# A spectral and FFN block: leftover rows of a DFT on 32-row tiles, a mirrored weight, and new orders of work

## The chip, the cores and the metric

The kernel runs on one core of a Trainium2 chip. Its engines work side by side, each on its own queue of instructions in program order: TensorE (PE) multiplies matrices, VectorE (DVE), ScalarE (ACT) and GpSimd (POOL) work element by element, and SyncE (SP) issues most of the DMA transfers. A matmul first loads its stationary operand, the weights, into the array (PEld in the profile), then streams the moving operand through it, and leaves its result in PSUM. Another engine has to copy it out to SBUF before the next stage can use it; these copies are called evictions here. The metric is the device time of one execution in microseconds (us).

## The reference

One block with a modulation: two halves, each a normalization, an affine from the condition `c`, a transform, and a gated sum.

```python
mod = (silu(c) @ w_mod).reshape(c.shape[0], 6, 1, -1)
sa, ca, ga, sb, cb, gb = (mod[:, i] for i in range(6))
h = layernorm(x) * (1 + ca) + sa
x = x + ga * irfft2(rfft2(h) * (w_r + 1j * w_i))
h = layernorm(x) * (1 + cb) + sb
x = x + gb * ((silu(h @ w_gate) * (h @ w_up)) @ w_down)
```

`x` is 1 x 2048 x 640 (S x D) in bf16, the transforms run over both axes, so the spectrum is 2048 x 321. The FFN is 1728 wide. The sums run in float32, tables and intermediate values are bf16.

## The kernel before

The two-dimensional transform is cut into small ones. D = 640 is 5 x 128: 128 positions with five residues r, and for the frequencies 65 columns l. S = 2048 is 16 tiles of 128 rows. The kernel has four stages, and the order inside each of the first three is a string of steps, `plan`, written by hand: each word is a function and a unit number, and the steps are issued to their engines in that order.

**Phase 1** (lines 268 to 415) works on 16 tiles t of x. `T` transposes a tile on TensorE (`turn`, L283), `h` copies it out (L286), `G` multiplies it by itself for the variance (L290), `d`, `p` and `r` make the reciprocal deviation, `s` scales the table G by it (L310, mostly POOL), `B` is the DFT along D (L317), `Z` its eviction with the mean taken out (L322, DVE), `S` the DFT along the rows of a tile (L330, L331) and `A` its eviction into `A_sb` (L335, ACT). `A_sb` holds, for each of the 65 columns l, NI = 160 numbers (tile, real or imaginary part, r). `ca` and `cb` scale the DFT table by the modulation; `ms` (L375), `sacs` (L379), `mh` (L386 to L390) and `sh` (L395) make the transform of the shift sa, `dsa`, which has five rows.

**The seam.** Phase 2 needs `A_sb` the other way round, in units u of four columns l: 4 x 160 = 640 values, or five blocks of 128, in `B2all`. Units 0, 1 and 16 are transposed on TensorE (`T` L436, `t` L442), units 2 to 15 by seven DMA transposes of two units each (`B`, L429), which SP issues. Since 160 is more than 128 rows, a column's values lie over two blocks, and each unit has its own cuts at rows 32, 64 and 96.

**Phase 2** (lines 417 to 627) is the short DFT across the tiles, the product with w_r and w_i, and the way back. For unit u, `X` (`stage_x`) multiplies the five blocks by ten variants of a table K: two matmuls of 320 columns (L456, L457), two small ones of ten by the weight `first`, which add the shift `dsa` (L459), and four of 160 (L461 to L464). Where a block holds parts of two columns, zero rows in K cut them apart. `Xe` evicts X (L471, ACT). `P` multiplies by the weights in one function, first 48 rows from `Wb`, then 32 from `Wq` (both at L489, DVE). `Y` sums the products with a unit matrix as weights (L503, L507) and `y` evicts it (L514), `E` is the inverse short DFT (L525 to L538) and `e` its eviction into `Ep` (L543, L548). `m` writes mirrored negative columns of `Ep` (L264, DVE).

`Wq` is W with its rows mirrored across partitions: `J` multiplies `Wb` by an exchange matrix `jrev` on TensorE (L585), `Je` copies it out (L588), `Jn` negates a third part. The mirror along l isn't done there: `P` reads `Wq` with a step of -1 along its last axis. `W0` to `W3` write the negative of `Wb` in four pieces of columns (L264). All these steps stand in the plan of phase 2, between `T`, `X` and `B`.

**Phase 3** takes the spectral output back to rows: `s` (`s1inv`, L646), `V` (its eviction, L653), `d` (`dinv`, L659), `x` (the sum with x, L662), then the second normalization (`n`, `q`, L666 and L670), `T` (turns in pairs), `f` (affine, L702 and L704). `sb`, `cb` and `mb` are the last three columns of the modulation, 25 small matmuls each (L231), and `sx`, `cx`, `mx` their evictions. The first units of the FFN (`gA`, then `g`, `z`, `m`) are interleaved at the end.

**The FFN** (from `ffn13` L725 and `ffn_mm` L738 on) multiplies by the gate and up weights, applies Silu on ACT (L743), the product on DVE (L747), and multiplies by the down weights (L860). The last 64 of 1728 rows, `down13` (L847), run on 64-row tiles of the array, where two matmuls can lie side by side. The end of the output has two matmuls at L857.

Phases 2 and 3 share four PSUM slots of two banks each (`slot`, `ring`). A step that needs a slot waits for the eviction of the one that had it.

Loads are issued by SP in the order of lines 188 to 211, before all plans:

```python
for g in range(0, NT, 2):
    if g:
        nc.sync.dma_start(x_sb[:, g:g + 2, :], x_v[:, g:g + 2, :])
    if g:
        nc.sync.dma_start(Gtab[:, g - 2:g], G_dram[:, g - 2:g])
```

and then `w_sa`, W, K, KI, eight small loads that replace parts of row 0 of W, the weights of the gate ga, and Rinv.

Of the kernel before, what the change touches and what calls it, by code (L numbers as in the profile page):

```python
# [19 lines left out]
NI = 160  # L20
# [10 lines left out]
def _tables():  # L31
# [16 lines left out]
    T["G"] = (5 * np.stack([np.cos(g), -np.sin(g)], axis=2)).astype(_NPBF)  # L48
# [29 lines left out]
    K = np.zeros((128, 17, NI))  # L78
    M = fwd(F)
    for v, (p0, p1, i0) in enumerate(((0, 128, 0), (0, 32, 128), (32, 128, 0), (0, 64, 96),  # L80
                                      (64, 128, 0), (0, 96, 64), (96, 128, 0), (0, 128, 32))):
        K[p0:p1, v] = M[i0:i0 + p1 - p0]
    turn = np.exp(-2j * np.pi * np.arange(NR) / 10.0)
    M = fwd(F * turn)
    K[96:128, 8], K[:, 9] = M[0:32], M[32:160]
    I = inv(F, (1, 1, 1, 1, 1))
    K[:, 10] = I[0:128]
    K[:, 11] = inv(F, (0.5, 1, 1, 0, 0))[0:128]
    K[:, 12] = inv(F * turn, (1, 1, 0.5, 0, 0))[0:128]
    for j in range(4):  # L90
        K[j::4, 13 + j] = I[128:160]
    ph = 2 * np.pi * np.outer(np.arange(NR), np.array([2, 1, 0, 3, 4])) / 5.0
    ph64 = ph + (2 * np.pi * np.arange(NR) / 10.0)[:, None]
    cs = np.stack([np.cos(ph), np.sin(ph), -np.sin(ph), np.cos(ph64), -np.sin(ph64)], axis=1)
    T["K"] = np.concatenate([K[:, :10].reshape(128, -1), np.broadcast_to(cs.reshape(1, -1), (128, 125)), np.zeros((128, 3))],
                            axis=1).astype(_NPBF)
    T["KI"] = np.ascontiguousarray(K[:, 10:]).astype(_NPBF)
# [4 lines left out]
NK = 10 * NI + 128  # L102
# [3 lines left out]
def adaln_block_kernel(  # L106
# [26 lines left out]
    Kv = Ktab[:, 0:10 * NI].rearrange("p (v q) -> p v q", q=NI)  # L133
    cs_v = Ktab[:, 10 * NI:10 * NI + 125].rearrange("p (r f) -> p r f", r=NR)
# [10 lines left out]
    rstd1 = const.tile([P, NT], F32, name="rstd1")  # L145
# [4 lines left out]
    sacs = const.tile([P, NR, 25], BF16, name="sacs")  # L150
# [8 lines left out]
    HB = 12  # L159
    early = big.tile([P, 2 * NC5 * D + HB * 660 + D], BF16, name="early", tag="ep")  # L160
    wm_ca = early[:, 0:NC5 * D].rearrange("p (k n) -> p k n", n=D)
    wm_sa = early[:, NC5 * D:2 * NC5 * D].rearrange("p (k n) -> p k n", n=D)
    hT_all = early[:, 2 * NC5 * D:2 * NC5 * D + HB * 660].rearrange("p (b r q) -> p b r q", b=HB, r=NR)
    c_row = early[0:1, 2 * NC5 * D + HB * 660:]
# [8 lines left out]
    Wq = big.tile([P, 3 * NT * 128 + 4], BF16, name="Wq", tag="wq")  # L173
    Wbr = Wb[:].rearrange("p a k (m l) -> p (a k m) l", m=3)
    Wqp = Wq[:, 0:3 * NT * 128].rearrange("p (a q) -> p a q", a=3)
    Wqr = Wq[:, 0:3 * NT * 128].rearrange("p (r l) -> p r l", l=64)
# [7 lines left out]
    nc.vector.memset(Wq[:, 3 * NT * 128:], 0.0)  # L184
    nc.vector.memset(Wqp[:, 1, 0:2048:64], 0.0)
# [4 lines left out]
    nc.sync.dma_start(x_sb[:, 0:2, :], x_v[:, 0:2, :])  # L190
    nc.sync.dma_start(wm_ca[:, 0:4], wm_v[:, 0:4, D:2 * D])
    nc.sync.dma_start(Rp, R_dram)
    nc.sync.dma_start(wm_ca[:, 4:5], wm_v[:, 4:5, D:2 * D])
    for g in range(0, NT, 2):
        if g:
            nc.sync.dma_start(x_sb[:, g:g + 2, :], x_v[:, g:g + 2, :])
        if g:
            nc.sync.dma_start(Gtab[:, g - 2:g], G_dram[:, g - 2:g])
    nc.sync.dma_start(Gtab[:, NT - 2:NT], G_dram[:, NT - 2:NT])
    nc.sync.dma_start(wm_sa, wm_v[:, :, 0:D])  # L200
    ws = [w.rearrange("(k2 k1) l -> k1 k2 l", k1=P) for w in (A_w_i, A_w_r)]
    for a in (1, 0):
        nc.sync.dma_start(Wb[:, a, :, 0:321], ws[a])
    nc.sync.dma_start(Ktab[:], K_dram)
    nc.sync.dma_start(KIt[:], KI_dram)
    for a in (1, 0):
        for m in (65, 193):
            for lo, hi, k in ((0, 15, 1), (15, 16, 0)):
                nc.sync.dma_start(Wb[0:1, a, lo:hi, m:m + 63], ws[a][0:1, k:k + hi - lo, m:m + 63])
    nc.sync.dma_start(wm_g[:, :, 0:D], wm_v[:, :, 2 * D:3 * D])  # L210
    nc.sync.dma_start(Rinv_sb[:], Rinv_dram)
# [8 lines left out]
    nc.gpsimd.memset(first[0:NR, 0:1], float(S))  # L220
# [5 lines left out]
    nc.scalar.activation(warm[:], eps_t[:], ACT.Silu)  # L226

# [32 lines left out]
    def negate(lo, hi, eng):  # L260
        eng(Wbr[:, 96:144, lo:hi], Wbr[:, 0:48, lo:hi])

# [3 lines left out]
    A_sb = big.tile([P, NL, NT, 2, NR], BF16, name="A_sb", tag="a")  # L266
    A_fl = A_sb[:].rearrange("p l t c r -> p (l t c r)")
    with tc.tile_pool(name="ph1", bufs=3) as ph1, \
# [4 lines left out]
        nc.gpsimd.memset(ones[:], 1.0)  # L273
        nc.vector.memset(Gt[:, 130:131], 1.0)
# [10 lines left out]
        def turned(t):  # L285
            (nc.vector.tensor_copy if t in HT_DVE else nc.scalar.copy)(hT_all[:, t % HB, :, 0:128], held.pop(("t", t)))  # L286

        def sums(t):
            for r in range(NR):
                nc.tensor.matmul(Gt[:, 0:130], lhsT=hT_all[:, t % HB, r, 0:128], rhs=hT_all[:, t % HB, r, 0:130],  # L290
                                 start=(r == 0), stop=(r == NR - 1))
# [15 lines left out]
        def gscale(t):  # L307
            Gss[t] = ph1.tile([P, 3, 128], BF16, name="Gs", bufs=6)
            e = nc.vector if t in S_DVE else nc.gpsimd
            e.tensor_scalar(Gss[t][:, 0:2], Gtab[:, t], rstd1[:, t:t + 1], None, ALU.mult)  # L310
            e.tensor_scalar(Gss[t][:, 2], Gtab[:, t, 1], rstd1[:, t:t + 1], -1.0, ALU.mult, ALU.mult)

        def dfwd(t):
            z = hold("z")
            held["z", t] = z
            for r in range(NR):
                nc.tensor.matmul(z[:, 128 * r:128 * r + 128], lhsT=hT_all[:, t % HB, r, 0:128], rhs=Rs[:, r, :],  # L317
                                 start=True, stop=True)
# [14 lines left out]
        def acopy(t):  # L333
            i = held.pop(("a", t)).rearrange("p (c x) -> p c x", c=2)[:, :, 0:325].rearrange("p c (r l) -> p l c r", r=NR)
            (nc.vector.tensor_copy if t in A_DVE else nc.scalar.copy)(A_sb[:, :, t, :, :], i)  # L335
# [42 lines left out]
        def sa_cs(_):  # L378
            nc.vector.tensor_tensor(sacs[:], cs_v, cps.unsqueeze(2).to_broadcast([P, NR, 25]), ALU.mult)  # L379

        def mod_sahat(_):
            sv = sacs[:].rearrange("p r (f m) -> p r f m", f=5)
            for cc, a, b, e in ((0, 0, 1, 3), (1, 2, 0, 4)):
                o = Tt[0:NR, 340 + NL * cc:340 + NL * cc + NL]
# [7 lines left out]
        def sa_out(_):  # L392
            sh = Tt[0:NR, 340:340 + 2 * NL].rearrange("p (c l) -> p c l", c=2).unsqueeze(2).to_broadcast([NR, 2, NR, NL])
            e5 = identb[0:NR, 0:NR].unsqueeze(1).unsqueeze(3).to_broadcast([NR, 2, NR, NL])
            nc.vector.tensor_tensor(dsa[0:NR, :, :, 0:NL], sh, e5, ALU.mult)  # L395

        HT_DVE, A_DVE, S_DVE, T_RING = (0,), (), (14,), (1, 3)
        GROUP = {0: 2, 2: 2, 4: 2, 6: 2, 8: 2, 10: 2, 12: 2, 14: 2}
        plan = (
# [549 lines left out]
```

## Time and profile before

| what | us |
|---|---|
| runs: lowest, median, highest of three | 269.31, 269.8, 271.63 |
| profiled execution, first to last instruction | 267.3 |
| phase 1 from the first full TensorE work (10.24 to 33.30): TensorE busy | 22.72 of 23.06 |
| FFN (85.50 to 264.00): TensorE busy | 178.50 of 178.50 |
| last copy and store (264.00 to 267.30): TensorE busy | 0.01 of 3.30 |

Of the profiled execution only the span is given; its own device time is not listed apart from it. The granted clock of TensorE was 0.999 over the whole span. The times of one stage are read like this: the windows give busy time per engine in a stretch, and what is missing to the stretch's length on TensorE is time in which it stood. The chain of waits then says which engine or transfer it stood for. In phase 1 DVE was busy for 20.75 us, ACT for 18.25 and POOL for 18.02 of 23.06 us.

### The profile page before, as it was taken

How to read it: one execution, taken by the hardware profiler on the slowest of the kernel's cores; microseconds unless marked ns; L12 is line 12 of the kernel's file. 1: busy time of each engine (PE TensorE's matmuls, PEld its weight loads, DVE VectorE, ACT ScalarE, POOL GpSimd, SP SyncE). 2: the span in 40 equal slices, each digit the busy share in tenths (PEclk: the TensorE clock that was granted, in tenths of full speed). 3: DMA queues.
4: the chain of work that ended last, by engine and by line, in shares of the span. 5: the costliest groups of instructions: out<-in, count | busy, mean ns of one | idle time of the engine just before them, and what ended most of it. 6: DMA issues, size and time to landing. Idle time of an engine off the chain costs nothing.

```text
span 267.3 us, 5300 instructions
## 1 busy us (share of the span) xinstructions
PE 258.3 (97%) x2180; PEld 166.6 (62%) x2180; DVE 148.3 (56%) x335; ACT 120.3 (45%) x216; POOL 26.0 (10%) x53
## 2 busy tenths in 40 slices
PE   6899999999989999999999999999999999999995
PEld 5688868998987445466644447654445664444663
DVE  2799989999598377773333352523344442333152
ACT  5599678988797598230122223022222203222000
POOL 3378800000010011100000000000000000000000
PEclk9999999999999999999999999999999999999999
DMA  7999399993696100050100013110005021000011
GB/s 252 325 332 326 111 271 172 308 395 111 196 379 218 35 13 0 0 98 28 64 19 12 0 33 65 53 59 10 2 0 98 3 73 34 10 2 0 0 52 49
DMA packets 36734, 28.12 MB, mean 105 GB/s; under 512 B 19429, under 2 KB 34022, under 8 KB 36582
## 3 DMA queue, kind: packets, MB, share of 16 engines
q1 hardware_dynamic: 36698, 27.79, 35.6%
q8 instruction: 17, 0.28, 0.4%
q14 instruction: 7, 0.06, 0.1%
q10 hardware_dynamic: 12, 0.00, 0.0%
HBM read 20.37 MB, written 2.62 MB: 86 GB/s over the span
## 4 chain that ended last, share of the span: by engine, by line
PE 86%; DMA 4%; ACT 3%; DVE 3%; SPq 2%; issue 1%; ACTq 0%
PE gu L738 42%; PE oa L860 21%; DMA x_sb<-in_A_x_dram 2%; PE yps L503 2%; DVE late L662 2%; DMA B2all<-A_sb 2%; PE gu L725 2%; PE z L317 2%; PE aps L330 2%; PE t1ps L283 1%; PE aps L331 1%; PE va L646 1%; PE gps L290 1%; PE mg_ps L231 1%; SPq L429 1%; PE oa L847 1%
## 5 line engine op out<-in xcount | busy, mean ns | idle before, releaser
L747 DVE TENSOR_TENSOR AT<-gu,sg 128x512 bf16<-128x512 f32 x52 | 35.9, 690 | 62.2 <-ACT sg L743 62.2
L738 PE MATMUL gu<-h2T_all,Wg 128*128 128x512 bf16 x260 | 64.6, 379 | 0.0
L738 PE MATMUL gu<-h2T_all,Wu 128*128 128x512 bf16 x260 | 64.6, 379 | 0.0
L743 ACT ACTIVATE sg<-gu 128x512 f32<-128x512 f32 x52 | 31.0, 597 | 69.8 <-PE gu L738 69.6
L860 PE MATMUL oa<-late,AT 128*128 128x320 bf16 x403 | 56.1, 299 | 0.0
L860 PEld LDWEIGHTS <-AT 128*128 128x128 bf16 x429 | 40.8, 98 | 17.2 <-issue 1.4
L738 PEld LDWEIGHTS <-Wu 128*128 128x128 bf16 x260 | 25.4, 98 | 30.7
L738 PEld LDWEIGHTS <-Wg 128*128 128x128 bf16 x260 | 25.1, 98 | 29.3
L874 DVE TENSOR_TENSOR xo<-oa,late 128x320 bf16<-128x320 f32 x31 | 20.0, 694 | 29.8 <-PE oa L847 16.7
L727 ACT ACTIVATE sg<-gu 64x512 f32<-64x512 f32 x4 | 2.4, 590 | 36.2 <-PE gu L725 36.2
L662 DVE SCALAR_TENSOR_TENSOR late<-oab,x_sb 128x640 bf16<-128x640 f32 x16 | 13.9, 890 | 4.8 <-PE oab L659 4.7
L310 POOL TENSOR_SCALAR Gs<-Gtab,rstd 128x256 bf16<-128x256 bf16 x15 | 13.9, 928 | 10.4 <-DVE rstd L305 9.1
L322 DVE SCALAR_TENSOR_TENSOR Z<-rtile,vm,z 128x640 bf16<-128x640 f32 x16 | 13.9, 872 | 0.4 <-PE z L317 0.3
L670 ACT ACTIVATE junk<-late,mean 128x640 bf16<-128x640 bf16 x16 | 13.3, 832 | 0.3
L471 ACT CAST X<-xps 128x640 bf16<-128x640 f32 x16 | 10.7, 696 | 3.3 <-PE xps L464 2.3
L335 ACT CAST A_sb<-aps 128x650 bf16<-128x650 f32 x16 | 11.1, 706 | 2.5 <-PE aps L331 2.3
L286 ACT COPY early<-t1ps 128x640 bf16<-128x640 bf16 x13 | 9.0, 692 | 4.6 <-PE t1ps L283 4.3
L646 PE MATMUL va<-Htab,Ep 128*128 128x128 bf16 x160 | 10.6, 219 | 0.3 <-DVE late L662 0.2
L653 ACT CAST VT<-va 128x640 bf16<-128x640 f32 x16 | 10.5, 705 | 0.5 <-PE va L646 0.4
L646 PEld LDWEIGHTS <-Ep 128*128 128x128 bf16 x160 | 9.7, 118 | 0.6 <-issue 0.5
L503 PE MATMUL yps<-identb,PP 128*128 128x128 bf16 x130 | 9.8, 219 | 0.0
L330 PE MATMUL aps<-Z,Gs 128*128 128x325 bf16 x32 | 9.2, 303 | 0.0
(287 smaller groups left out, 333.8 us busy)
## 6 DMA issues: line engine op xcount, KB each, us to landing
x_sb<-in_A_x_dram SPq DMA_DIRECT2D x8, 320.0 KB, 6.4
out_dram<-xo SPq DMA_DIRECT2D x15, 160.0 KB, 1.8
Wu<-in_B_w_up_dram SPq DMA_DIRECT2D x1, 2080.0 KB, 10.3
late<-in_B_w_down_dram SPq DMA_DIRECT2D x1, 2080.0 KB, 16.5
wm_g<-in_w_mod_dram SPq DMA_DIRECT2D x2, 800.0 KB
Wb<-in_A_w_r_dram SPq DMA_DIRECT2D x1, 1284.0 KB, 11.0
Wb<-in_A_w_i_dram SPq DMA_DIRECT2D x1, 1284.0 KB
Wg<-in_B_w_gate_dram SPq DMA_DIRECT2D x1, 1280.0 KB
```

What stands on the lines that cost most here:

```text
L310: e.tensor_scalar(Gss[t][:, 0:2], Gtab[:, t], rstd1[:, t:t + 1], None, ALU.mult)
L322: nc.vector.scalar_tensor_tensor(Zs[t][:].rearrange("p r q -> p (r q)"), rv, vm[:, t, 1:2], held.pop(("z", t))[:, 0:D], ALU.mult, ALU.add)
L330: nc.tensor.matmul(o, lhsT=Gs[:, a, :], rhs=Z[:, :, 0:NL], start=True, stop=False)
L503: nc.tensor.matmul(yf[:, 128 * j:128 * j + 128], lhsT=PP[:, cp, 0:128] if u == 16 else PP[:, cp, 0:128, j], rhs=identb[:], start=(cp == 0) ...
L646: nc.tensor.matmul(vf[:, 128 * r:128 * r + 128], lhsT=Ep[:, t, 65 - 65 * g:193 - 65 * g, r], rhs=Htab[:, t, g, :], start=(f == 1 and r in ...
L662: nc.vector.scalar_tensor_tensor(x1[:, t, :].rearrange("p (r a) -> p r a", r=NR), VTs.pop(t).rearrange("p (r a) -> p r a", r=NR), 1.0, x_s ...
L670: nc.scalar.activation(junk[:], x1[:, t, :], ACT.Square, scale=-1.0 / D ** 0.5, bias=mean2[:, t, 1:2], accum_out=sq2[:, t:t + 1])
L738: nc.tensor.matmul(o, lhsT=w_[:, c5, fc * 128:(fc + 1) * 128], rhs=h2T_all[:, sc % 2, :, c5, :], start=(c5 == 0), stop=(c5 == NC5 - 1))
L743: nc.scalar.activation(gus[fc][1][:], gus[fc][0][:, 0, :], ACT.Silu)
L747: nc.vector.tensor_tensor(AT[:, fc, :], gu[:, 1, :], sg[:], ALU.mult)
L860: nc.tensor.matmul(o, lhsT=AT[:, fc, tl * 128:(tl + 1) * 128], rhs=Wd_sb[:, fc, h * 320 + d0:h * 320 + d0 + n], start=(fc == 0 and not ear ...
L874: nc.vector.tensor_tensor(xos[tl][:, h * 320:(h + 1) * 320].rearrange("p (a r) -> p a r", r=NR), ps[0][0].rearrange("p (a r) -> p a r", r= ...
```

## The change

**Blocks.** `A_sb` is cut into `A_main`, which holds 128 of a column's 160 values, and `A_rest`, which holds the other 32. `A` writes tiles 0 to 11 into the one and 13 to 15 into the other, and tile 12 by three copies. A unit is then four blocks of 128 in `Bm` and one block in `Bl`, where the 32 leftover rows of four columns lie on top of each other. The DMA transposes of `Bm` have 8 blocks, not 10; two more, `Bl2` (6 blocks) and `Bl8` (8 blocks), bring the leftovers of units 2 to 15. `t` makes two copies.

**X.** `X` takes two units at once, in two PSUM slots. The table K shrinks from ten variants to four.

```diff
+            other = pss["x", u + 1] = slot("xps")
+            for h in range(2):
+                for j in range(4):
+                    mm((xps, other)[j // 2][:, j % 2, NI * h:NI * h + NI], lhsT=Bm[:, (u + h) % 8, j], rhs=Kv[:, 0, :], start=(h == 0), stop=False)
+            for h in range(3):
+                for j in range(4):
+                    g, o = slice(32 * j, 32 * j + 32), (xps, other)[j // 2][:, j % 2, :]
+                    if h == 0:
+                        mm(o[:, 0:2 * NI].rearrange("p (h c q) -> p h c q", h=2, c=2)[:, :, :, 45:50], lhsT=first[g, :],
+                           rhs=dsa[g, :, :, 4 * u + j:4 * u + j + 5:4].rearrange("p c m h -> p h c m"), start=False, stop=False)
+                    else:
+                        mm(o[:, NI * (h - 1):NI * h], lhsT=Bl[g, u + h - 1, :], rhs=Kv[g, 1, :], start=False, stop=(h == 2))
```

That is eight matmuls of 160 columns on the full array, then twelve on 32 rows, in three rounds of four row groups. `first` and `dsa` are repeated in four groups of 32 rows for this: the weights of `mh` are widened from 5 to 128 columns (`sacs` writes 500 values a partition, not 125, into a cleared tile), and `sh` works on 128 partitions with a mask. `Xe u` now evicts one of the two slots, that is two columns of each unit, so a `P` needs both evictions of its pair. X is stored as one tile for two units.

**The mirrored weight.** `J` moves from phase 2 into phase 1 and reads the moving columns backwards, so that `Wq` is mirrored along l too:

```diff
-                nc.tensor.matmul(ps[:, b, :], lhsT=jrev[:], rhs=wv[:, 8 * (h % 2) + 4 * b:8 * (h % 2) + 4 * b + 4, :, 64:128], start=True, stop=True)
+                nc.tensor.matmul(held["j", h][:, 512 * b:512 * b + 512], lhsT=jrev[:],
+                                 rhs=wv[:, 8 * (h % 2) + 4 * b:8 * (h % 2) + 4 * b + 4, :, 127:63:-1], start=True, stop=True)
```

The product is cut into two steps, `P` (48 rows from `Wb`) and `R` (32 rows from `Wq`), and `R` reads with a step of +1. The negations `W0` to `W3` and `Jn` become `N0` and `N1`, 8 x 321 values a partition each, and `N2`, 2048 values:

```diff
+        def negate(i):
+            if i == 2:
+                neg_dve(held["wq"][:, 0], held["wq"][:, 2])
+            else:
+                neg_dve(Wb[:, 2, 8 * i:8 * i + 8, 0:321], Wb[:, 0, 8 * i:8 * i + 8, 0:321])
```

**Loads.** They become steps of the plans. In the order of the queue: x0, ca (four of five parts), x2, ca (the rest), R, x4, G0, x6, G2, G8, x8, x12, x10, G4, x14, G10, G12, G6, W real, W imaginary, one small load of row 0, sa, G14, two small, K between five more small ones; in phase 2 ga, B2, Bl2, B4, Bl8, KI, B6, B8, H, B10, Rinv, B14, B12, sb, Wu, the second half of `wm_g`. The table G is stored so that a load of two tiles is one piece. The copies of turned x in `hT_all` are kept for all 16 tiles, not in a ring of 12, and part of the modulation weights lie where `Wq` will be.

**Engines of the evictions.** One list names those on DVE, all others are on ACT:

```python
ON_DVE = set("Je0 Xe0 Xe8 Xe10 Xe13 Xe14 e12 e16 g15 h0 h4 t1 t16 y2 y4 y14".split())
```

Before, X was evicted on ACT, Y on DVE but for seven odd units, E on ACT but for unit 14 and half of 15, and of J two on DVE.

**Plans.** All three strings are new. The end of phase 1, then the beginning of phase 2, before and after:

```diff
-            "A12 S13 A13 S14 A14 sh S15 A15 "
+            "... s14 Z15 ms1 s15 S13 S14 sacs S15 A13 J2 "
+            "A14 mh N1 A15 J3 J0 N0 Je2 Je3 sh Je0 J1 Je1 N2 "
...
-            "W0 J3 W1 T0 Je3 J2 J0 Je2 t0 Je0 T1 B2 X0 t1 Xe0 ga Jn J1 X1 X2 B4 Xe1 Je1 P0 Xe2 X3 gt X4 Xe3 B6 X5 Y0 P1 Xe4 "
+            "T0 lga t0 T1 ga B2 Bl2 t1 X0 Xe0 X2 Xe1 R1 B4 P1 X4 Xe3 P0 R0 Xe2 Y1 Xe4 y1 Bl8 P3 P2 R2 lKI Xe5 Y0 R3 y0 E1 e1 P4 B6 "
+            "gt B8 Y2 E0 y2 Y3 X6 L3 R4 e0 y3 Y4 R5 P5 Xe6 y4 E2 Xe7 B10 Y5 e2 R6 P6 R7 lRi E3 y5 e3 X8 Y6 E5 Xe8 E4 P7 Xe9 R9 y6 "
```

At the end of phase 2 it now reads `E14 E15 e12 e14 e15 m4 wm m3`: the step `wm`, which loads ACT's table for Silu, stands behind the last eviction of E (before: ahead of `e14`, `e16` and `e15`). Phase 3 begins `sb sx cb s0 s2 cx s1 V0 V2 V1 d0` where it began `sb sx cb cx s0 s1 s2 V0 d0`, has `mb` and `mx` ahead of the turns `T0` and `T1` where they stood between `f1` and the first step of the FFN, `gA` (L725), and has `gA` itself behind the units 2 and 5 of the FFN, and takes the first FFN units in the order 2, 5, 6, 0, 4, 3, 1, 7.

More of the change, by code (lines that the diff above doesn't have):

```diff
@@ L149, in adaln_block_kernel @@
     sc_col = const.tile([P, NC5], BF16, name="sc_col")
-    sacs = const.tile([P, NR, 25], BF16, name="sacs")
+    mask5 = const.tile([P, NR], F32, name="mask5")
     dsa = const.tile([P, 2, NR, 68], BF16, name="dsa")
@@ L219, in adaln_block_kernel @@
     nc.gpsimd.memset(first[:], 0.0)
-    nc.gpsimd.memset(first[0:NR, 0:1], float(S))
+    for g in range(4):
+        nc.gpsimd.memset(first[32 * g:32 * g + NR, 0:1], float(S))
     nc.gpsimd.memset(dsa[:], 0.0)
@@ L522, in stage_e @@
             Y2 = Y2s.pop(u)
-            mm = nc.tensor.matmul
             if u == 16:
```

261 lines of the change are left out of this document (133 added, 128 removed), and 27 rows, old and new, of the table plan.

## The prediction

> **What bounds the kernel now.** The first view is the page's busy table, and then the windows by stage (columns: time, PE, PEld, DVE, ACT, POOL busy with instruction counts, clock, DMA share, GB/s).
>
> ```profile
> PE 258.3 (97%) x2180; PEld 166.6 (62%) x2180; DVE 148.3 (56%) x335; ACT 120.3 (45%) x216; POOL 26.0 (10%) x53
> ```
> ```profile
> 0.00:10.24 10.24, 7.26 (x85) 6.18 (x86) 4.32 (x27) 5.80 (x10) 3.56 (x18) 1.00 0.79 255
> ...
> 33.30:42.30 9.00, 8.21 (x104) 6.23 (x101) 7.81 (x14) 6.73 (x12) 0.00 (x0) 1.00 1.14 235
> 42.30:66.90 24.60, 24.25 (x334) 21.95 (x335) 23.32 (x45) 22.25 (x38) 0.00 (x0) 1.00 0.86 256
> 66.90:85.50 18.60, 17.32 (x311) 16.35 (x311) 14.16 (x40) 16.11 (x33) 1.27 (x2) 1.00 0.84 283
> ```
>
> The reader sees a TensorE with nearly no holes at full clock. Idle are 3.0 us before 10.24, 0.8 at the seam (33.3 to 42.3), 0.35 in the spectral stage (42.3 to 66.9) and 1.3 in stage three (66.9 to 85.5); after that the FFN runs, which the change leaves alone. So time can come from TensorE work taken away before 85.5, or from the holes. In the spectral stage DVE (23.3 of 24.6) and ACT (22.3) are nearly as full, so shorter PE work is worth its length only if both get lighter too. The second view is the chain of waits (start, length, what), which says who ends each hole.
>
> ```profile
> 3.60 6.59 DMA x_sb<-in_A_x_dram
> ...
> 27.05 0.36 PE t1ps L375 x10
> ...
> 31.03 0.15 PE t1ps L388 x5
> ...
> 32.40 1.92 ACT A_sb L335 x3
> 34.37 1.46 SPq L429
> ...
> 37.45 4.83 DMA B2all<-A_sb
> 42.33 0.31 PE xps L456
> ...
> 66.97 2.15 PE mg_ps L231 x50
> 69.12 1.69 PE va L646 x30
> ...
> 84.53 0.94 PE mg_ps L231 x25
> ...
> 86.55 0.28 PE oab L659 x5
> ...
> 116.26 7.06 PE oa L860 x52
> ```
>
> The holes are a late load of x (until 10.24), the transposes of A by DMA (until 42.33), and in stage three the chain from the spectral output through ACT and DVE to the first FFN matmul, at 84.53 + 0.94 = 85.47.
>
> **X on tiles.** Cadence is read from starts, since a matmul's own length overlaps the next. The chain in the spectral stage:
>
> ```profile
> 43.13 0.14 PE xps L456
> ...
> 43.68 0.07 PE xps L464
> 43.75 0.45 PE yps L503 x8
> ```
>
> One unit of X takes 43.75 - 43.13 = 0.62 us, a pair 1.24. The new pair has eight full-array matmuls of 160 columns (0.07 each: 0.56) and twelve on 32 rows: four of 20 columns, eight of 160. No 32-row tile is in this trace; the nearest row is the 64-row one of the FFN (timeline: start, length):
>
> ```profile
> 123.02 0.30 PE L860 MATMUL oa<-late,AT 128*128 128x320 bf16 x1
> 123.25 0.72 PE L847 MATMUL oa<-late,AT 64*128 64x320 bf16 x8
> 123.90 0.58 PE L860 MATMUL oa<-late,AT 128*128 128x320 bf16 x3
> ```
>
> A full 320-column matmul takes 7.06/52 = 0.136. Eight 64-row ones take 0.65, where eight in turn would take 1.09: they run in pairs (4 x 0.136 = 0.54), and going in and out costs 0.23 - 0.136 = 0.09 and 0.65 - 0.54 = 0.11. So the tiled part costs 0.20 of switching, plus, at best, three groups of four at once (0.04 + 2 x 0.07 = 0.18), or, if each of the twelve takes what a matmul with a new full-width weight and almost no columns takes (0.36/10 = 0.036, L375), 0.43. The pair is 0.94 to 1.19. I take 1.06, the middle, as nothing is nearer: 0.18 saved on each of eight pairs, **-1.4 us** (-2.4 to -0.4 if tiles overlap). Two worse bounds: twelve in turn (4 x 0.04 + 8 x 0.07 = 0.72) give 1.48, or +1.9; loads at the most that L847 allows, two in 0.136, hence 12 x 0.068 = 0.82, give 1.58, or +2.7. A rule speaks against the change: the Trainium skill, "TensorE: Matmul & The Clock Gate", section "LDWEIGHTS (loading the stationary operand)", says that a 32x128 load takes as long as a 128x128 one, columns over 1.2 GHz, an estimated 107 ns, by which the pair would be 2.04 and the stage 6 us longer. The trace here caps a load at 68 ns.
>
> **DVE and ACT in that stage** (timeline):
>
> ```profile
> 39.17 0.55 DVE L489 TENSOR_TENSOR PP<-X,Wb 128x768 bf16<-128x768 bf16 x1
> 39.63 0.59 DVE L489 TENSOR_TENSOR PP<-X,Wq 128x512 bf16<-128x512 bf16 x1
> 40.14 0.55 DVE L489 TENSOR_TENSOR PP<-X,Wb 128x768 bf16<-128x768 bf16 x1
> ...
> 42.06 0.81 DVE L514 CAST Y<-yps 128x640 bf16<-128x640 f32 x1
> 42.79 0.54 DVE L489 TENSOR_TENSOR PP<-X,Wb 128x768 bf16<-128x768 bf16 x1
> ```
> ```profile
> 47.83 0.72 ACT L548 CAST Ep<-eps__1068 128x640 bf16<-128x640 f32 x1
> 48.43 0.74 ACT L548 CAST Ep<-eps__1077 128x640 bf16<-128x640 f32 x1
> ```
>
> The reversed 512 elements keep DVE 0.51, more than 768 forward ones (0.46); forward, 512 of 768 should cost some 0.35, so DVE wins 16 x 0.15 = 2.4 (none, if the reversal is not the cause). An eviction costs DVE 0.73, ACT 0.60, by the starts of neighbours. The X copies now write with steps of four elements, where E's, at 0.60, write runs of five: I count no more for them; twice the time would make ACT the bound by some 11 x 0.6. DVE gives up six full and one small y for five X, one or two pieces of E: about -1; ACT gives up five X and takes six y, about +1. Lists after: DVE 16 x (0.46 + 0.35) + nine evictions at 0.73 + some 4 small = 23.5, ACT some 37 evictions at 0.60 + 2 = 24, over a stage of some 27 us from X0. Both stay below PE (16 Y at 0.56, 16 E at 0.55, 8 X at 1.06: 26.3). So PE's saving counts, if its four PSUM slots do not run out, as a pair of X takes two.
>
> **Front.** TensorE's first long stand, to 10.24, is for x4 (two tiles, 327 kB). In the old queue one load of two G tiles (128 x 512 elements of two bytes, 131 kB) stood ahead of it that now follows: at 255 GB/s 0.5 us earlier. Bounds: 0, if the root of the variance or R is late next, and 1.0, if the other G load that moves behind x also stood in its way. The gain counts only where the work behind it follows at once, and it arrives at the seam, where I book it.
>
> **The seam.** Its rows (timeline):
>
> ```profile
> 30.07 0.29 DVE L379 TENSOR_TENSOR sacs<-Ktab,t1ps 128x125 bf16<-128x125 bf16 x1
> ...
> 33.22 0.84 DVE L264 TENSOR_SCALAR Wb<-Wb,neg 128x816 bf16<-128x816 bf16 x2
> ...
> 35.70 1.23 DVE L588 CAST Wq<-wps 128x1024 bf16<-128x1024 f32 x1 [0.32 <-PE wps L585]
> 36.84 0.48 DVE L442 COPY B2all<-t2ps 128x640 bf16<-128x640 bf16 x1
> 37.24 0.74 DVE L264 TENSOR_SCALAR Wq<-Wq,neg 128x2048 bf16<-128x2048 bf16 x1
> ```
> ```profile
> 46.37 0.30 PE L456 MATMUL xps<-Ktab,B2all 128*128 128x320 bf16 x1
> ...
> 66.39 0.23 PE L538 MATMUL eps__1472<-KIt,Y 128*128 128x160 bf16 x1
> ...
> 69.72 2.65 ACT L653 CAST VT<-va 128x640 bf16<-128x640 f32 x4 [0.39 <-PE va L646]
> ```
> ```profile
> DMA to landing us min/median/max: 3.5/3.6/4.8
> ```
>
> The last line is the transposes' own (B2 to B14). The last copy of A ended at 34.32. With 0.5 from the front and sacs (0.2) behind the last Z, it ends at 33.6, and B2 is issued then. B2 now has 8 blocks and not 10. B2 landed 34.37 + 3.6 = 38.0, and B6, two further on, 37.45 + 4.83 = 42.28: ten blocks take 2.1 once flowing, of 3.6 with the start. 8 should take 1.7, the new Bl2 (6 blocks) 1.3, so B2 lands near 36.7, Bl2 38.0, B4 39.7, and behind Bl8 and KI (0.28 MB, 0.9) B6 44. So much for the transposes; the other line to the first X runs over DVE. All turning of W (J, Je and N) now stands in phase 1, ahead of T0, the first transpose on TensorE. T0's PSUM slot comes free with sh, T1's with the copy Je0, and both, with the negations, are in one DVE queue: N1, N0, sh, Je0, N2, t1. The first can start when the last row of W fixed by its own small load has landed, near 33 as now (the negation at 33.22 was the one that waited for it). N1 and N0 have 2568 elements each: 0.74 x 2568 / 2048 = 0.93 by the row at 37.24, say 0.9; at most twice that, if the odd row length of 321 halves the rate. They end at 34.8; sh (as many elements a partition as an eviction, 0.75) at 35.5; Je0 (1.23) at 36.7; N2 (0.74) at 37.4; t1 (0.48 and its small second copy) at 38.0. X0, which now needs both units, starts at 38.0, X2 at 39.1, X4 at 40.1: none waits for its transposes, all stand behind DVE. Before, two X units had run by then, but X6 stood until 42.33. After it, going down the plan with the durations above: Y1 at 41.3, E1 when y1 is out, X6 when y2 is out, and X7 is through at 46.2, with Y0 to Y3, E0 and E1. Before had that much done when the X at 46.37 began: 0.1 to 0.2 is won. The 30 matmuls of mh have weights of 128 columns and not 5: 30 x (0.036 - 0.030) = 0.2, hidden under the wait for DVE. So **-0.1** for the seam, front included (between +1.6, N at half rate, and -1.0, the whole of the front and sooner DVE). From there four pairs save 4 x 0.18 = **0.7**. The last matmul of E ended at 66.39 + 0.07 = 66.46 and now ends 0.8 earlier, at 65.7.
>
> **Stage three.** Now sb and cb (2.15) run ahead of s0 at 69.12. After it sb, s0, s2, cb: s0 waits for the mirrors (a copy out and two negations like those of 0.73 above: 1.5 behind the last E), and cx, ahead of V0 on ACT, waits for cb behind s2. V0, the copy out of s0, starts 1.5 + 0.3 + 0.55 (ten of L646's 0.056) + 1.1 + 0.2 = 3.6 behind the last E; before it was 69.72 - 66.46 = 3.3. So **+0.3**. The Silu table load, off the path of the last copy of E, is hidden under this. V0 starts 0.5 earlier, and ACT's list from V0 to f1 is the same. The gb matmuls (0.94) stood between f1 and the first FFN matmul (84.53 to 85.47) and now stand earlier, in a hole: **-0.9** (0, if their load of weights is late). One dinv (0.28) less is left: **-0.3**. Wm_g's second half is now loaded behind Wu, cover for it is the stretch to cb at 68; gone, it costs the lateness in full.
>
> **The sum** on the profiled 267.3 span: -0.1 - 0.7 + 0.3 - 0.9 - 0.3 = -1.7. The runs' median of 269.8 lies 2.5 above that span, which I leave: **268.1 us**. The 1.4 of X is not all in it, as half the pairs run while PE waits for DVE.
>
> **The rivals.**
> Faster: tiles overlap in full, (1.24 - 0.94) x 8 = -2.4, and the front's 0.5 and the seam's 1.0 come through: 268.1 - 1.0 - 1.5 = 265.6. For it speaks that PE is the fullest engine; against, the DVE queue at the seam.
> Slower, by weight loads: a 32-row group is paced by its loads at 0.068 each, the pair takes 1.58. X then costs +2.7 in place of -1.4 over eight pairs, and 268.1 + 4.1 = 272.2; it decides from 0.04 us a load on, where a pair passes 1.24. That L847's loads keep pace with its 0.136 speaks against; that nothing shows four in 0.07, for.
> Slower, by reversed columns: the two L857 matmuls, whose moving operand steps over 128 elements, take some 0.26 for 160 columns (261.43 to 261.97 in the chain below).
>
> ```profile
> 261.43 0.54 PE ob L857 x2
> ```
>
> At that rate eight W matmuls of 512 take 0.86 and not 0.22: +5.1, ahead of T0, so 273.3. Here the step is -1, next to 1; unlikely.
> No gain: each transpose costs 2.1 whatever its blocks, Bl2 and Bl8 push B6 to some 47.3, and X6 stands 1.5 longer: 269.7.
>
> **Chances.** The sum 0.35; faster rival 0.33; no gain 0.16; loads 0.10; columns 0.06. The measurement tells about 1% from no change, 2.7 us either way: the bounds are 267.1 and 272.5. Faster by over 1%: the faster rival and little of the sum's lower edge, 0.35. Slower: columns, and half of the loads with a late seam, 0.12. The rest, 0.53, is within. The range leaves out the columns and the corners: 264.6 to 272.0; the sum's own is 266.8 (the rest of the seam's 1.0, and the tiles' best on four pairs, 4 x 0.12, less what DVE still hides) to 269.7 (N at half rate).
>
> **What would show it.** Right: the X pair at 1.0 to 1.1 between starts, tile matmuls of one group nanoseconds apart; R products near 0.35; X0 at 38; first FFN matmul near 84. Wrong: PE waiting in the spectral stage for X copies (slots), W matmuls above 0.22, B transposes ending PE's waits, or cb waiting for its load.

## The result, and the profile after

The changed kernel takes 279.68 us (median; 278.76 to 280.51), the kernel before 269.56 (268.60 to 271.63) beside it: a ratio of 1.0376, with a 95% interval of 1.0337 to 1.0414. That is 10 us more, where 268.1 was forecast. The profiled execution took 280.51 us, with a span of 278.7.

The page of the changed kernel, its busy table, the granted clock in 40 slices, and one of its groups (busy time in us, mean ns of one, idle time before):

```profile
PE 261.3 (94%) x2212; PEld 167.6 (60%) x2212; DVE 151.4 (54%) x332; ACT 129.4 (46%) x220; POOL 29.7 (11%) x58
...
PEclk9999998699999999999999999999999999999999
...
L519 ACT CAST X<-xps 128x640 bf16<-128x640 f32 x11 | 17.0, 1646 | 1.5 <-PE xps L509 1.5
```

The same group on the page of the kernel before:

```profile
L471 ACT CAST X<-xps 128x640 bf16<-128x640 f32 x16 | 10.7, 696 | 3.3 <-PE xps L464 2.3
```

Two things are new. A copy of X on ACT takes 1.65 us where it took 0.70, for the same 640 values; and the clock has a hole. The windows of the changed kernel (columns as in the prediction) say where TensorE lost its time:

```profile
33.00:42.00 9.00, 8.41 (x135) 6.29 (x132) 7.41 (x12) 6.69 (x12) 1.16 (x2) 1.00 0.69 127
42.00:70.00 28.00, 22.07 (x301) 18.21 (x294) 19.78 (x39) 25.90 (x33) 0.00 (x0) 0.88 0.77 181
...
45.00:48.00 3.00, 1.00 (x13) 0.69 (x12) 1.70 (x4) 3.00 (x4) 0.00 (x0) 0.82 1.07 327
48.00:51.00 3.00, 2.97 (x22) 2.40 (x21) 1.08 (x2) 2.41 (x4) 0.00 (x0) 0.50 0.92 249
51.00:54.00 3.00, 3.00 (x36) 2.51 (x35) 1.44 (x4) 1.55 (x4) 0.00 (x0) 0.54 0.00 0
```

In the spectral stage ACT is the full engine now (25.9 of 28.0 us), and TensorE stands for 5.9. The timeline of TensorE puts nine of its stands (times in which it waits) between 42 and 73 us, 5.2 us together, down to copies of X. Two of them:

```profile
42.86 0.71 PE L501 MATMUL xps<-Ktab,B_all 128*128 128x160 bf16 x8 [0.77 <-ACT X L519]
...
45.76 0.61 PE L554 MATMUL yps<-identb,PP 128*128 128x128 bf16 x8 [0.73 <-ACT X L519]
```

From 45 to 48 us TensorE works for one of three; then it is granted half its clock for six, and looks busy because its matmuls take longer: in the chain of waits below, eight matmuls of Y take 1.01 us at 49.21, and 0.45 at 64.97. The same chain has six X copies on ACT between 54 and 73 us, 9.1 us together, four of them in these lines:

```profile
49.21 1.01 PE yps L554 x8
...
53.96 3.02 ACT X L519 x2
...
62.59 1.52 ACT X L519
...
64.97 0.45 PE yps L554 x8
...
66.82 1.58 ACT X L519
```

The timeline of TensorE gives the ends of the stages (start, length), the last matmul of E and the first of the FFN:

```profile
77.01 0.23 PE L588 MATMUL eps__1504<-KIt,Y 128*128 128x160 bf16 x1
...
96.25 1.02 PE L775 MATMUL gu<-h2T_all,Wg 128*128 128x512 bf16 x4 [0.96 <-DVE mean L703]
```

The last matmul of E starts at 77.01, before at 66.39, and the first FFN matmul at 96.25, before at 85.31. The profiled spans differ by 11.4 us (278.7 and 267.3; the changed kernel's profiled execution is the longest of its four): 10.6 of them are ahead of the last E, and the stage behind it gives nothing back.

### The profile page after: what moved, and what is told of

Same layout as the page of the kernel before. It is cut to its first block, busy times and chain, and to the rows that moved or that the text cites. A ratio compares the mean times of both kernels' runs of the same rounds, so it can differ in the third digit from the quotient of the medians.

```text
span 278.7 us, 5367 instructions
## 1 busy us (share of the span) xinstructions
PE 261.3 (94%) x2212; PEld 167.6 (60%) x2212; DVE 151.4 (54%) x332; ACT 129.4 (46%) x220; POOL 29.7 (11%) x58
## 4 chain that ended last, share of the span: by engine, by line
PE 70%; ACT 10%; issue 1%; DVE 1%; ACTq 0%
PE gu L775 40%; PE oa L896 20%; ACT X L519 3%; ACT VT L690 2%; PE gu L762 2%; PE yps L554 1%; ACT junk L707 1%; ACT Y L565 1%; PE oa L883 1%; ACT Ep L598 1%; PE va L683 1%; PE mg_ps L231 1%; PE ob L896 1%; PE xps L501 1%; ACT h2T_all L739 1%
## 5 line engine op out<-in xcount | busy, mean ns | idle before, releaser
L896 PEld LDWEIGHTS <-AT 128*128 128x128 bf16 x429 | 40.8, 98 | 17.2 <-issue 1.4
L519 ACT CAST X<-xps 128x640 bf16<-128x640 f32 x11 | 17.0, 1646 | 1.5 <-PE xps L509 1.5
L554 PE MATMUL yps<-identb,PP 128*128 128x128 bf16 x130 | 10.8, 230 | 2.3 <-ACT X L519 2.2
L683 PE MATMUL va<-Htab,Ep 128*128 128x128 bf16 x160 | 10.6, 219 | 0.7 <-ACT VT L690 0.5
L554 PEld LDWEIGHTS <-PP 128*128 128x128 bf16 x130 | 9.2, 118 | 3.3 <-issue 2.7
L350 ACT CAST A_sb<-aps 128x650 bf16<-128x650 f32 x15 | 10.4, 708 | 1.6 <-PE aps L337 1.3
L287 ACT COPY early<-t1ps 128x640 bf16<-128x640 bf16 x12 | 8.3, 692 | 5.9 <-PE t1ps L284 5.9
```

What stands on the lines that cost most here:

```text
L519: evict("Xe%d" % u)(Xs[u // 2][:, :, :, j0:j0 + 2].rearrange("p h q j -> p j h q"), xps[:, :, 0:2 * NI].rearrange("p j (h q) -> p j h q", ...
L554: nc.tensor.matmul(yf[:, 128 * j:128 * j + 128], lhsT=PP[:, cp, 0:128] if u == 16 else PP[:, cp, 0:128, j], rhs=identb[:], start=(cp == 0) ...
L683: nc.tensor.matmul(vf[:, 128 * r:128 * r + 128], lhsT=Ep[:, t, 65 - 65 * g:193 - 65 * g, r], rhs=Htab[:, t, g, :], start=(f == 1 and r in ...
L896: nc.tensor.matmul(o, lhsT=AT[:, fc, tl * 128:(tl + 1) * 128], rhs=Wd_sb[:, fc, h * 320 + d0:h * 320 + d0 + n], start=(fc == 0 and not ear ...
```

## The experiments

**The copies of X, and the clearing of sacs.** The first theory is that the form of the copy costs the time. The old copy went through the four columns of a unit innermost and wrote runs of four values; the new one goes through the rows innermost and writes single values, four apart. The second suspicion comes from DVE's timeline at the start, in the kernel before and in the changed kernel, with POOL's of the changed kernel behind them:

```profile
2.87 0.31 DVE L371 CAST sc_col<-sc_f 128x5 bf16<-128x5 f32 x1 [1.15 <-ACT sc_f L369]
4.44 0.49 DVE L286 COPY early<-t1ps 128x640 bf16<-128x640 bf16 x1 [1.25 <-PE t1ps L283]
```

```profile
2.88 3.91 DVE L386 CAST sc_col<-sc_f 128x5 bf16<-128x5 f32 x1 [1.14 <-ACT sc_f L384]
4.78 2.01 DVE L287 COPY early<-t1ps 128x640 bf16<-128x640 bf16 x1
```
```profile
2.71 0.67 POOL L191 MEMSET dsa<- 128x680 bf16 x1
...
3.98 2.77 POOL L273 MEMSET sacs<- 128x3200 bf16 x1
```

In the changed kernel the two DVE operations take 3.91 and 2.01 us, where they took 0.31 and 0.49. Both end at 6.79, and POOL's clearing of `sacs`, the last of eight clearings that follow each other from 2.71 on, ends at 6.75. Four kernels were run for the two suspicions, all on one chip, with the kernel before beside them. The first is the changed kernel with its copies in runs of two:

```diff
-            evict("Xe%d" % u)(Xs[u // 2][:, :, :, j0:j0 + 2].rearrange("p h q j -> p j h q"),
-                           xps[:, :, 0:2 * NI].rearrange("p j (h q) -> p j h q", h=2))
+            evict("Xe%d" % u)(Xs[u // 2][:, :, :, j0:j0 + 2],
+                           xps[:, :, 0:2 * NI].rearrange("p j (h q) -> p h q j", h=2))
```

> The changed kernel, with the X copies going through the columns in another order: the two columns of one slot innermost, so that each write is a run of two elements (4 bytes) and not of one. Theory A, the copy's single-element writes cost the time (an X copy took 1.65 us on ACT and 1.60 on DVE where the old form took 0.70): the copy falls to 0.7 to 0.85, ACT is no longer full between 42 and 70 us, TensorE doesn't stand long enough there for its clock to fall, and 8 to 9.5 of the 10 us lost come back: 270 to 272. Rival B, the pair of units itself (two slots per X, both copies needed before a product) or the clock: the copies get faster or not, but the time stays above 276. Rival C, the longer time of the copy comes from reading PSUM bank after bank and not from the writes: the copy stays at 1.6.

The second is the kernel before, with its copy in the new form:

```diff
-            nc.scalar.copy(X[:].rearrange("p q (b j) -> p q b j", b=2),
-                           xps[:, :, 0:2 * NI].rearrange("p b (j q) -> p q b j", j=2))
+            nc.scalar.copy(X[:].rearrange("p q (b j) -> p b j q", b=2),
+                           xps[:, :, 0:2 * NI].rearrange("p b (j q) -> p b j q", j=2))
```

> The kernel before, with its X copies in the column order of the changed kernel: written one element at a time with a step of four. Nothing else differs. Theory A: each of 16 copies takes 1.6 us on ACT, 0.9 more; ACT had 22.25 of 24.6 us in the spectral stage, so it becomes the bound there and the time rises by 9 to 14 us, to 279 to 283.5. Rival B (pair and clock are the cause): the copy stays at 0.7, or its length is hidden, and the time stays within 271.

The third is the changed kernel with `sacs` cleared on DVE, and the fourth has both edits:

```diff
-        nc.gpsimd.memset(sacs[:], 0.0)
+        nc.vector.memset(sacs[:], 0.0)
```

> The changed kernel, with the 3200 elements of sacs cleared by DVE (idle from 1.7 to 2.9 us) and not by POOL. Theory D: DVE's small cast at 2.88 took 3.91 us, and its copy of turned x 2.01, because both ended with POOL's clearing (3.98 to 6.75); without it the cast takes 0.3, the first sum of squares starts near 5.3 and not 6.86, and the end of phase 1 moves up by 1.0 to 1.6 us (last copy of A out at 34.3 to 34.9, was 35.9). The time falls by 1 to 1.6 to about 278.3. Rival E, the order of the loads is what made phase 1 late: the cast gets short, the end of phase 1 stays within 0.4 us, the time stays.

> The changed kernel with both edits, X copies in runs of two and sacs cleared by DVE. Theory A with D: 268.5 to 270.5, about the time before. If the copies in pairs cost as little as the old ones and nothing else is slow, what the tiles save (an X pair takes 0.92 on TensorE, was 1.24: 8 x 0.3 = 2.5) and the forward products show as well: 266 to 268. Rival B: above 274.

| kernel | us, median | ratio to before | 95% interval |
|---|---|---|---|
| changed | 279.68 | 1.0376 | 1.0337 to 1.0414 |
| X copies in runs of two | 271.20 | 1.0067 | 1.0037 to 1.0097 |
| kernel before, X copies of single values | 279.39 | 1.0360 | 1.0323 to 1.0396 |
| sacs cleared on DVE | 277.91 | 1.0300 | 1.0264 to 1.0336 |
| both edits | 269.90 | 1.0019 | 0.9987 to 1.0052 |

The first row is the result from above; each ratio goes by the kernel before that ran beside it. The copy's form is shown to be the cause from both sides: with it undone 8.5 us of the 10 come back, and put alone into the kernel before it costs 10. The view by tile of the first run (duration min/median/max in ns, first and last start in us):

```profile
L519 ACT CAST X<-xps x11: 692/696/738, 40.8 to 61.7; 128x640 bf16<-128x640 f32 x11
L519 DVE CAST X<-xps x5: 816/825/826, 40.8 to 61.7; 128x640 bf16<-128x640 f32 x5
```

and the group on the page of the second:

```profile
L471 ACT CAST X<-xps 128x640 bf16<-128x640 f32 x16 | 24.9, 1682 | 1.9 <-PE xps L464 1.2
```

Runs of two values cost as little as runs of four, 0.70 on ACT; single values cost 1.68. The slow form reads PSUM along rows, the fast ones jump between columns and banks, so it isn't the reading: the copies of `VT`, which read along rows as well and write whole rows, take 0.70 too (705 ns on the page of the kernel before). The same holds for DVE (0.83 against 1.60). Single values at another step than 8 bytes were not run, so whether the single 2-byte write or its step is dear stays open.

The clearing is shown too. In the third run DVE's first operations (timeline) and ACT's last copy of A are

```profile
3.28 0.81 DVE L386 CAST sc_col<-sc_f 128x5 bf16<-128x5 f32 x1
...
5.49 0.49 DVE L287 COPY early<-t1ps 128x640 bf16<-128x640 bf16 x1 [1.39 <-PE t1ps L284]
```
```profile
32.54 1.92 ACT L350 CAST A_sb<-aps 128x650 bf16<-128x650 f32 x3 [0.63 <-PE aps L337]
```

The cast does not come down to the 0.31 of the kernel before: it ends at 4.09, again with POOL's last clearing, which now ends at 4.06. The copies of A are out at 34.46; in the changed kernel they were at 33.98 + 1.92 = 35.90. That is 1.4 us, and 1.8 in the median. These are single executions: the first run, whose beginning is that of the changed kernel, has 35.49, and the fourth, whose beginning is that of the third, 33.42. The gain is clear of this spread, its size is not fixed to better than a microsecond.

**What is left.** The run with both edits is level with the kernel before, though its X is shorter on TensorE. In its profiled execution the last matmul of E starts at 65.58, 0.8 earlier than before, but phase 1 ended 0.9 earlier there too (33.42 against 34.32). Its timeline shows two stands of TensorE that the kernel before didn't have:

```profile
43.48 0.30 PE L583 MATMUL eps__999<-KIt,Y 128*128 128x320 bf16 x1 [1.34 <-ACT Y L565]
...
67.88 1.19 PE L231 MATMUL mg_ps<-sc_col,wm_g 128*128 128x64 bf16 x25 [1.09 <-DMA wm_g<-in_w_mod_dram]
```

The first is put down to a copy of Y that was done at 42.14; what came last was the table KI, whose load is issued at 37.90 behind four transposes. In the run below that moves only `wm_g`, the profile names this load itself for the same stand (0.93 us). The second is the late half of `wm_g`, issued behind Wu. And stage three has a new order. Each was undone alone in the run with both edits, then all together: `lKI` moved behind `lf5` in phase 1; `L4 Xe15 R12 L1` made `L1 L4 Xe15 R12`; and the plan of stage three replaced by the old string.

> The run with both edits (269.9), with the load of KI moved from its place behind four transposes of the seam to the end of phase 1, where the kernel before had it. In that run TensorE stood 1.55 us before E1, whose table had landed at 43.4. Theory F, the load sets the start of E: the stand falls to 0.3 to 0.7 (E1 then waits for its Y copy), and 0.8 to 1.5 us are won: 268.4 to 269.1. Rival G, E1 would have waited for ACT just as long: under 0.3 us won.

> The run with both edits (269.9), with the load of the second half of wm_g issued ahead of Wu and not behind it. There cb stood 1.29 us for it (to 67.88), and s0 behind cb. Theory H, this load is what ate the time that E wins (the last matmul of E ended at 65.6, before at 66.5): cb starts at 66.6, s0 at 67.8, and 0.9 to 1.3 us are won: 268.6 to 269.0. Rival I, s0 waits for the mirrored columns or ACT's list in stage three is full anyway: under 0.3 us.

> The run with both edits (269.9), with the order of stage three of the kernel before. There the first FFN matmul came 17.0 us behind the start of s0, before 16.4, and TensorE stood 0.93 us more at 91. Theory J, the new order of stage three is slower than the old: 0.6 to 1.6 us are won, 268.3 to 269.3. Rival K, as forecast, the new order saves by moving mb: the old one costs 0.3 to 0.9 more, 270.2 to 270.8.

> All three of these at once on top of the two edits. If the three waits lie one after the other: 265.5 to 267.5, faster than before by 0.7 to 1.4%. If TensorE's gain in the spectral stage is eaten by another wait each time: 268.5 to 269.5, no faster than before.

| kernel | us, median | ratio to before | 95% interval | last E | first s0 | first FFN matmul |
|---|---|---|---|---|---|---|
| before | 269.43 | | | 66.39 | 68.95 | 85.31 |
| both edits | 269.90 | 1.0019 | 0.9987 to 1.0052 | 65.58 | 68.90 | 86.09 |
| + KI early | 269.36 | 0.9987 | 0.9961 to 1.0013 | 64.81 | 68.22 | 85.41 |
| + wm_g first | 269.22 | 0.9988 | 0.9967 to 1.0009 | 65.30 | 67.35 | 84.54 |
| + old stage three | 268.26 | 0.9941 | 0.9909 to 0.9973 | 65.70 | 68.25 | 84.61 |
| + all three | 267.15 | 0.9915 | 0.9883 to 0.9946 | 65.16 | 67.22 | 83.59 |

The times of the last four rows were taken on another chip than those of both edits, with the kernel before beside them (269.43). The last three columns are starts in the timelines of TensorE, of one execution each, and by then phase 1 has ended as early as 33.42 or as late as 34.53, so the distance between two starts of one row says more than one column. With the early table E1 no longer stands, and the last E comes 26.6 us behind X0, where it came 27.9 behind it. With the earlier `wm_g` cb no longer stands, and s0 comes 2.1 behind the last E, where it came 3.3 behind it. In the medians the two win 0.5 and 0.7; their intervals overlap with that of both edits, so by the times alone neither is told from nothing. The old order of stage three is 1.6 faster than the new one (2.1 by the ratios), with an interval clear of that of both edits, against the forecast. All together make 267.15, 0.85% faster than the kernel before, inside the range for three waits that lie one after the other.

**The clock.** In the changed kernel, with nothing else undone, 48 matmuls whose results nobody reads (10 ahead of Y1, 14 ahead of Y0, 24 ahead of E1) fill the time in which TensorE waited:

```diff
+            for _ in range({1: 10, 0: 14}.get(u, 0)):
+                mm(yps[:, 1, 256:384], lhsT=identb[:], rhs=identb[:], start=True, stop=True)
...
+            for _ in range({1: 24}.get(u, 0)):
+                mm(eps_[:, 1, 416:512], lhsT=identb[:], rhs=identb[:, 0:96], start=True, stop=True)
```

> The changed kernel (279.7) with 48 extra matmuls of 128 or 96 columns whose results nobody reads: 10 ahead of Y1, 14 ahead of Y0, 24 ahead of E1, in PSUM columns that the stages don't use. They fill what TensorE waited there (0.7, 0.9 and 1.5 us). Theory L, the clock fell to half (granted 0.50 to 0.54 from 48 to 54 us) because TensorE had stood for most of 42 to 48, and this cost about 3 us on the path: the clock stays at 1.0, and the time is 276.5 to 278.2. Rival M, ACT's slow copies would have set the pace all the same: the clock stays up, and the time stays within 0.7 of 279.7. Rival N, so few matmuls don't hold the clock: it falls as before.

It took 278.17 us (ratio 1.0299, 1.0250 to 1.0348), and the windows show the clock held:

```profile
45.00:48.00 3.00, 2.83 (x53) 2.56 (x51) 1.70 (x4) 3.00 (x4) 0.00 (x0) 1.00 1.01 256
48.00:51.00 3.00, 2.85 (x41) 2.56 (x39) 1.99 (x5) 2.67 (x7) 0.00 (x0) 1.00 1.06 276
51.00:54.00 3.00, 2.45 (x42) 1.88 (x40) 1.35 (x3) 3.00 (x4) 0.00 (x0) 1.00 0.49 95
```

So the fall of the clock came from TensorE's idling. Holding it wins 1.5 us by the medians and 2.1 by the ratios, where about 3 were expected; what the extra matmuls cost themselves was not measured. With the clock held ACT is busy for 3.00 of 3.00 us in each stretch of three from 51 to 63, and the kernel is still 8.6 above the 269.55 of the kernel before beside it: that is the slow copies and the clearing, without any fall of the clock.

**The tiles.** From the run with all edits, X's twelve matmuls on 32 rows go back to the full array, with four more variants of K that have zero rows, and the shift through all 128 rows:

```diff
-                        mm(o[:, NI * (h - 1):NI * h], lhsT=Bl[g, u + h - 1, :], rhs=Kv[g, 1, :], start=False, stop=(h == 2))
+                        mm(o[:, NI * (h - 1):NI * h], lhsT=Bl[:, u + h - 1, :], rhs=Kv[:, 4 + j, :], start=False, stop=(h == 2))
```

> The run with all edits (267.15), with X's twelve matmuls on 32-row tiles made on the full array: four more variants of K with zero rows, and the shift added through all 128 rows, so eight full matmuls of 160 columns and four of 20 stand in place of the tiles. Blocks, pairs, copies and orders stay. Theory O, the tiles are worth what TensorE's starts say: the pair of X takes 1.26 (16 x 0.07 + 4 x 0.036) and not 0.93, 8 x 0.33 = 2.6 us, of which those count that don't lie in the wait for DVE at the seam: 268.6 to 269.8. Rival P, TensorE's shorter X is hidden behind DVE and ACT, so the tiles are worth nothing: within 0.4 of 267.15.

It took 269.09 us (0.9980, 0.9954 to 1.0005), 1.9 more than with tiles (1.8 by the ratios, whose intervals don't overlap). Its timeline, and that of the run with tiles:

```profile
46.43 0.72 PE L504 MATMUL xps<-Ktab,B_all 128*128 128x160 bf16 x8
46.98 0.32 PE L509 MATMUL xps<-dsa,first 128*128 128x20 bf16 x4
47.13 0.73 PE L512 MATMUL xps<-Ktab,B_all 128*128 128x160 bf16 x8
47.69 0.61 PE L557 MATMUL yps<-identb,PP 128*128 128x128 bf16 x8
```
```profile
45.48 0.72 PE L501 MATMUL xps<-Ktab,B_all 128*128 128x160 bf16 x8
46.13 0.20 PE L506 MATMUL xps<-dsa,first 32*128 32x20 bf16 x4
46.16 0.30 PE L509 MATMUL xps<-Ktab,B_all 32*128 32x160 bf16 x8
46.40 0.64 PE L554 MATMUL yps<-identb,PP 128*128 128x128 bf16 x8
```

A pair takes 47.69 - 46.43 = 1.26 without tiles and 46.40 - 45.48 = 0.92 with them: 0.34 eight times is 2.7, of which 1.9 reach the end. Without the tiles the kernel can't be told from the kernel before, so of all that the change does, the tiles carry most of the gain; what the mirrored weight and the halved products are worth by themselves no run shows.

**The front.** Two more, from the run with all edits: the clearing on DVE moved behind the cast of the modulation's input, and then, with that, the loads put back in the old order.

> The run with all edits (267.15), with the clearing of sacs on DVE moved behind the cast of the modulation's input. There it stood from 1.93 to 3.32 and held back that cast (ended 4.08) and TensorE's first matmuls (x's first transpose at 4.7, in the kernel before at 3.7). If the start sets the pace of phase 1: 0.3 to 0.7 won, 266.4 to 266.9. If the loads of the modulation's weights (ca's last part stood to 9.3) set it: nothing won, within 0.3 of 267.15.

> The run with all edits and the later clearing (266.87), with the first 32 loads issued in the order of the kernel before, x and G by turns and R ahead of the second x, all ahead of the plan of phase 1; the order of that plan itself stays the new one. Theory Q, as forecast for the front, x ahead of G wins 0.5 (0 to 1.0): 267.2 to 267.8. Rival R, the order of loads is worth nothing, since the modulation's weights and their cast set the start: within 0.25 of 266.87. Rival S, the new plan of phase 1 asks for its tables at other times, and the old order makes it stand: over 268.

They took 266.87 (0.9878, 0.9837 to 0.9920) and 266.77 us (0.9923, 0.9893 to 0.9953). Neither can be told from 267.15 (0.9915). Between the two the old order of loads is 0.1 faster by the medians and 1.2 slower by the ratios, with intervals that overlap; so whether x ahead of G wins 0.5 stays open.

## Why the prediction was wrong

**The step that failed** is the sentence on the copies: "The X copies now write with steps of four elements, where E's, at 0.60, write runs of five: I count no more for them; twice the time would make ACT the bound by some 11 x 0.6." The step was seen, its bound was named, and then it was neither in the sum, nor in the range, nor a rival. Only the list of signs had it ("PE waiting in the spectral stage for X copies (slots)"), and this sign came, 0.77 by the row at 42.86. E's row was no evidence: its runs of five say nothing of runs of one. A copy of X measured 1646 - 696 = 0.95 more on ACT, eleven times, and 0.77 more on DVE, five times; that is more than the doubling which was the worst that was thought of. With 10.4 us more, the prediction's own list of ACT goes from 24 to 34, where TensorE's has 26.3, and 8.5 us came back when the copies alone were undone. The sentence behind it, "Both stay below PE", held only with the old copy. A cost bounded at +6.6 belonged in the range, which would then have reached to 274.7; it ended at 272.0, and the measured cost lies beyond both.

**The second miss** is the front: 0.5 was to be won, and 1.6 were lost (A out at 35.90, before 34.32). What was not costed is an operation that the change adds on an engine that seemed idle, POOL's clearing of 3200 elements, and who waits for it. With it gone, phase 1 ends between 33.42 and 34.53 in the seven profiled executions that clear `sacs` on DVE ahead of the cast, about where it ended before; the load order won nothing that the runs can tell.

**Stage three** was read wrongly. The plan says `sb sx cb s0`, so cb runs ahead of s0 as it did before, not behind `s2`. The 0.9 of mb was to be won because its matmuls leave the place ahead of the first FFN matmul, while "ACT's list from V0 to f1 is the same". They left it, but the list did not stay the same: from s0 to the first FFN matmul the run with both edits takes 17.2 us (68.90 to 86.09), where the kernel before took 15.6 to the start of mb (68.95 to 84.53) and 16.4 with mb. The old order, with mb in its old place, is 1.6 faster than the new one. All of the order was put back at once, so no run says which of its steps costs this. That the late half of `wm_g` "costs the lateness in full" showed in the run with both edits: TensorE stood for it, 1.09 by its row. In the changed kernel itself, where this stage begins more than 11 us later, cb ran straight behind sb (78.06 behind 77.08).

**The seam.** X0 was forecast at 38.0 and came at 40.16. The front explains most of it: with the clearing gone X0 comes at 37.68 in the run with both edits and at 38.53 in the run with all edits. No X waits for its transposes, as forecast; but that X4 would wait for a copy of X, and, with the copies in pairs, E1 for KI, which is now queued behind the transposes, was not seen.

**What held.** The X pair was put at 0.94 to 1.19, and 1.06 was taken; it measured 0.92, so the tiles overlap in full, and the rival that said so was right on this point. The rival of weight loads paced at 0.068 each is out. The reversed columns of `J` cost nothing (two matmuls of 512 in 0.45, the rows below), so that rival is out too. The two halves of a product behave as forecast: R now takes 43.21 - 42.87 = 0.34, was 0.51. The long negations took 1.69 for two, forecast 0.9 each. The rule of the Trainium skill ("TensorE: Matmul & The Clock Gate", section "LDWEIGHTS (loading the stationary operand)") is out as a price for tiles one after another: by it the pair would be an estimated 2.04, and the trace has 0.92.

The timeline of the changed kernel for these:

```profile
34.89 0.61 PE L418 MATMUL wps<-Wb,jrev 128*128 128x512 bf16 x2
35.34 0.35 PE L402 MATMUL t1ps<-rtile,sacs 128*128 128x64 bf16 x5
```
```profile
34.70 1.69 DVE L261 TENSOR_SCALAR Wb<-Wb,neg 128x2568 bf16<-128x2568 bf16 x2
...
42.87 0.43 DVE L541 TENSOR_TENSOR PP<-X,Wq 128x512 bf16<-128x512 bf16 x1
43.21 1.02 DVE L541 TENSOR_TENSOR PP<-X,Wb 128x768 bf16<-128x768 bf16 x2
```

The chance of 0.12 for slower was given for none of the causes that made it so. And it is in part luck that the run with all edits, 267.15, lies near the forecast of 268.1: the tiles gave more than was taken (0.32 a pair, not 0.18), and the 0.9 of stage three was not won, for in that run its old order is back.

So the change, with stage three left in its old order and two loads in time, holds a gain of about 1% (2.3 us against before in the run with all edits, 2.7 with the later clearing) behind two costs of 8.5 and 1.8 us that its idea doesn't need.

## What to carry to other kernels

When a layout changes, write down for every copy what its innermost loop writes, and price a run of one value by itself: here two values side by side cost 0.70 us and single ones 1.65 for the same 640. Count the clearing operations on POOL as work that DVE may wait for. And when an engine that feeds TensorE is nearly full, as ACT was with 22.3 of 24.6 us, a doubled copy on it is not a footnote but the forecast.

## What the runs showed of the hardware

Single bf16 values written four apart (8 bytes) cost 2.4 times as much as pairs on ACT (1.65 against 0.70) and 1.9 times on DVE (1.60 against 0.83). The Trainium skill ("SBUF — State Buffer", section "Door 1: The DMA port swizzle (why `[64,N]` ≈ `[32,N]`)") speaks of lines of 16 bytes that have to be hit at least twice, and names 8 bf16 values as the step that is still free. A step of four single values, which hits each line twice, isn't free here: for these writes the measurement decides.

A DVE cast of 5 values took 3.91 us, since it ended only with POOL's clearing; in the third run, with that clearing gone, it took 0.81, and ended again with POOL's last (4.09 and 4.06). The Trainium skill ("SBUF — State Buffer", section "Who interferes with whom") says that casts and copies of DVE can enter modes that share a port pair with GpSimd, and that the later one is blocked for a whole instruction. The rows agree in kind, both DVE operations end within 0.04 us of POOL's; which mode they ran in no trace shows. For how many clearings a copy waits differs: in the changed kernel the cast waited through all of POOL's from its start on, in the kernel before it ended at 3.18, while POOL's clearings went on to 3.41.

The clock fell to half although TensorE was not at rest: it had worked 1.00 of 3 us from 45 to 48, and came back to full speed about 6 us later. With the 48 extra matmuls, which made this 2.83 of 3 us, it stayed at 1.00.
